# TensorE no longer waits on its own semaphore in an attention-and-FFN block on one core

## Chip, core and metric

The kernel runs on one core of a Trainium2 chip. The metric is device time in microseconds (us); the median of three runs of the kernel before is 1126.47 us (1125.41 to 1128.68).

## What is computed

A pre-norm transformer block for one sequence of 2048 tokens, width 512, 32 heads of 16, and an FFN of 1792. Inputs and output are bf16.

```
h   = x + softmax((q k^T) * 16**-0.5) v @ wo     # q, k, v = split(layernorm(x) @ wqkv)
out = h + (gelu(z @ w_gate) * (z @ w_up)) @ w_down   # z = layernorm(h), gelu by tanh
```

## The kernel before, in words

**Queues and waits.** `Plan` records each engine's instructions in order. A buffer key has a last writer and its readers, each a pair of engine and count; an instruction that writes the key depends on all of them. `_waits_for` turns these into waits on the engines' progress semaphores and leaves out what the engine has waited for already. This holds for the engine's own earlier instructions too: a matmul that writes a PSUM bank (key `("pb", b)`) which an earlier matmul wrote waits until TensorE's own semaphore (`prog_pe`) shows that matmul as done. `group_begin` and `group_end` move the waits of a group of matmuls to its first one.

**The order.** `Sched` sets the order of every queue while the program is built: it plays the kernel with assumed durations (`TMM` for a 512-column matmul, `TTR` for a transpose, `TQK` and `TPV` for a step of scores and of P·V) and always takes the stream whose next operation can start first, within `LOOK` by priority. `_ready` adds `LAT` after the last operation that is depended on, also where that is one of the same engine.

**The steps.** The work is 32 units (4 chunks of 512 queries x 8 groups of 4 heads), each of 64 tiles of 128 keys x 512 queries, 2048 tiles in all.
- `qk` (recorded at L1147, tile names `QT,KT`): steps of three tiles into PSUM banks 0 to 2 and of two tiles into banks 3 and 4, in turn. A step waits until ScalarE has read the tiles that stood in its banks.
- `exps` (L1153): one exponential on ScalarE for each step: "wide", 1536 columns, for three tiles, "narrow", 1024, for two; 410 wide and 409 narrow ones. A wide and a narrow one together are called a pair here: five tiles.
- `pv` (L1147, `PT,VA`): four matmuls for four tiles, added up in bank 5 (`PVB`) over the 16 key steps of a unit. `ofin` copies that bank out (VectorE, `OA`, L1342), transposes it in two halves (L1346) and divides.
- Dense work in banks 6 and 7: projections (L1146) with transposes (L1229), per chunk the output projection with layer norm (`post`, L1383 to L1407), then `gates`, `ups` and `downs` (L1146). A projection, gate or up is two recorded operations of two matmuls on one bank; a down is 14 matmuls in five operations on one bank.
- Gelu of chunks 0 to 2: VectorE copies the gate (L1431), GpSimd does three operations (L1433 to L1435), ScalarE the tanh (L1441), VectorE two more. In chunk 3, after the last exponential, ScalarE does the whole gelu (L1447). That chunk's post, gates, ups and downs are called the tail.
- `fill` (L1510 to L1523): matmuls of zeros, put in where the plan sees TensorE idle and the columns of a running account (`RATE` per us) are owed. Most add zeros to bank 5, so a fill and a P·V step are writers of the same bank.

A second program with its own plan (`max_path`) stands behind a branch and is not run here.

Of the kernel before, what the change touches and what calls it, by code (L numbers as in the profile page):

```python
# [15 lines left out]
class Plan:  # L16
# [47 lines left out]
    def _waits_for(self, e, deps, extra=()):  # L64
        need = {}
        for (k, v) in list(deps) + list(extra):
            if k == e.name and v > e.count:
                continue
            if v > need.get(k, 0):
                need[k] = v  # L70
        waits = []
        for k, v in need.items():
            if e.known.get(k, 0) >= v:
                continue
            e.known[k] = v
            waits.append((k, v))
        self.n_waits += len(waits)
        return waits
# [800 lines left out]
class Sched:  # L879
# [30 lines left out]
    def _ready(self, op):  # L910
# [9 lines left out]
        if isinstance(op, Op):  # L920
            for k in op.writes:
# [3 lines left out]
                for tok in P.readers.get(k, ()):  # L925
                    r = max(r, self.done[tok])
        return r + LAT

# [7 lines left out]
    def _emit(self, op, start):  # L936
# [4 lines left out]
        for tok in extra:  # L941
            start = max(start, self.done[tok] + LAT)
        self.now = max(self.now, start)
# [64 lines left out]


IDLE = 90000  # L1010
LAT = 0.08
LOOK = 0.12
NRING = 30
NG = 3
TMM, TTR, TTR32, TQK, TPV = 0.24, 0.12, 0.26, 0.34, 0.33
SLOTS = ((0, 3), (3, 2))
PVB = 5
DENSE = (6, 7)
# [572 lines left out]
```

## Time and profile before

| | |
|---|---|
| median of the runs | 1126.47 us |
| profiled execution, its own time | 1128.3 us |
| its span, first to last instruction | 1126.6 us |
| first exponential starts, last one ends | 29.47 and 1054.66 us |
| busy share of the span: TensorE, ScalarE, VectorE, GpSimd | 90%, 88%, 23%, 16% |

The profiled execution lies 1.8 us above the median and 1.7 us above its own span. Times in rows count from the start of the span. "Idle before" at the end of a row is what the engine stood still ahead of that instruction, with the instruction that ended the wait. PE is TensorE's matmuls, PEld its weight loads, ACT ScalarE, DVE VectorE, POOL GpSimd.

### The profile page before, as it was taken

The numbers are of one execution on the slowest core, as the hardware profiler recorded it, in microseconds if no ns is written. First come the engines' busy times: TensorE is split into PE (matmuls) and PEld (weight loads), VectorE is DVE, ScalarE is ACT, GpSimd is POOL, SyncE is SP. The second block draws the span as 40 slices with busy tenths as digits, with TensorE's granted clock in tenths as the row PEclk, the third lists the DMA queues.
The fourth block names the chain that finished last, engine by engine and source line by source line (L and its number), as shares of the span: only waits on it lengthen the run. The fifth ranks groups of instructions, "written<-read, shape, count | busy, mean of one in ns | idle before, by whom it ended". The sixth has DMA issues, their size and how long they took to land.

```text
span 1126.6 us, 15044 instructions
## 1 busy us (share of the span) xinstructions
PE 1017.5 (90%) x6105; PEld 298.4 (26%) x6220; DVE 257.5 (23%) x462; ACT 987.4 (88%) x897; POOL 181.0 (16%) x191
## 2 busy tenths in 40 slices
PE   7899999898998998999899999899999998998887
PEld 2222222222222222222222222222222222222222
DVE  5343600000355200000245300000256200000332
ACT  3599999999999999999999999999999999999420
POOL 6500000000067200000058300000058200000000
PEclk9799999999999999999999999999999999999999
DMA  4000140000000000000000000000000000000000
GB/s 149 1 1 1 50 166 1 1 1 1 1 1 1 10 29 1 1 1 1 1 1 1 10 29 1 1 1 1 1 2 1 10 29 1 1 1 1 1 1 22
DMA packets 12847, 14.96 MB, mean 13 GB/s; under 512 B 1760, under 2 KB 11744, under 8 KB 12768
## 3 DMA queue, kind: packets, MB, share of 16 engines
q1 hardware_dynamic: 12768, 13.90, 3.7%
q8 instruction: 51, 0.84, 0.3%
q14 instruction: 28, 0.23, 0.1%
HBM read 11.80 MB, written 2.10 MB: 12 GB/s over the span
## 4 chain that ended last, share of the span: by engine, by line
PE 76%; POOL 8%; issue 6%; ACT 5%; DVE 2%; POOLq 0%; ACTq 0%; DVEq 0%
PE pbank L1147 34%; PE pbank L1513 23%; PE pbank L1146 15%; ACT PT L1153 5%; POOL w_sb L1435 3%; POOL w_sb L1433 2%; POOL w_sb L1434 2%; PE pbank L1523 2%; PE pbank L1346 2%; POOL xn_sb L1222 1%; DVE OA L1342 1%; DVE g_sb L1431 0%; PE pbank L1405 0%; PE pbank L1383 0%; DVE VA L1282 0%
## 5 line engine op out<-in xcount | busy, mean ns | idle before, releaser
L1153 ACT ACTIVATE PT<-pbank 128x1536 bf16<-128x1536 f32 (+1 forms) x819 | 949.4, 1245 | 55.4 <-PE pbank L1147 52.0
L1147 PE MATMUL pbank<-QT,KT 32*128 32x512 bf16 x2048 | 316.5, 385 | 19.5 <-ACT PT L1153 9.9
L1513 PE MATMUL pbank<-ones_bf,zero_bf 128*128 128x512 bf16 x707 | 275.4, 389 | 48.4 <-PE pbank L1147 15.3
L1147 PE MATMUL pbank<-PT,VA 128*17 128x512 bf16 x2048 | 202.1, 385 | 4.1 <-PE pbank L1147 0.8
L1342 DVE COPY OA<-pbank 128x512 f32<-128x512 f32 x32 | 22.1, 690 | 530.2 <-PE pbank L1147 530.2
L1147 PEld LDWEIGHTS pbank<-QT,KT 32*128 32x128 bf16 x2048 | 77.7, 91 | 240.2 <-issue 139.7
L1513 PEld LDWEIGHTS pbank<-ones_bf,zero_bf 128*128 128x128 bf16 x776 | 74.4, 96 | 246.5 <-PE pbank L1513 141.9
L1399 POOL TENSOR_SCALAR rstd_95<-mv_94 128x1 f32<-128x1 f32 x16 | 3.6, 224 | 834.8 <-DVE mv_94 L1397 834.8
L1147 PEld LDWEIGHTS pbank<-PT,VA 128*17 128x17 bf16 x2048 | 49.7, 87 | 124.4 <-PE pbank L1513 59.0
L1146 PE MATMUL pbank<-wd_sb,GUT 128*128 128x512 bf16 x213 | 59.2, 382 | 2.9 <-PE pbank L1147 0.6
L1435 POOL TENSOR_TENSOR w_sb<-w_sb,g_sb 128x512 f32<-128x512 f32 x42 | 55.5, 1321 | 3.5
L1433 POOL TENSOR_TENSOR w_sb<-g_sb 128x512 f32<-128x512 f32 x42 | 46.1, 1097 | 39.2 <-DVE g_sb L1431 39.1
L1447 ACT ACTIVATE w_sb<-pbank 128x512 f32<-128x512 f32 x14 | 8.4, 597 | 38.8 <-PE pbank L1146 38.8
L1146 PE MATMUL pbank<-xnT,wqkv_sb 128*128 128x512 bf16 x123 | 37.7, 391 | 1.7 <-DVE xnT L1236 0.5
L1442 DVE SCALAR_TENSOR_TENSOR w_sb<-w_sb,g_sb 128x512 f32<-128x512 f32 x42 | 33.7, 802 | 23.7 <-ACT w_sb L1441 23.3
L1431 DVE COPY g_sb<-pbank 128x512 f32<-128x512 f32 x42 | 28.9, 689 | 36.3 <-PE pbank L1146 36.3
L1434 POOL TENSOR_SCALAR w_sb<-w_sb 128x512 f32<-128x512 f32 x42 | 33.5, 797 | 3.7
L1467 DVE SCALAR_TENSOR_TENSOR GUT<-pbank,w_sb 128x512 bf16<-128x512 f32 x42 | 28.7, 688 | 23.3 <-PE pbank L1146 23.2
L1441 ACT ACTIVATE w_sb<-w_sb 128x512 f32<-128x512 f32 x42 | 26.7, 636 | 7.0 <-POOL w_sb L1435 6.9
L1346 PE MATMUL pbank<-ident_77,OA 128*128 128x128 f32 x128 | 27.9, 300 | 2.3 <-DVE OA L1342 2.1
L1523 PE MATMUL pbank<-ones_bf,zero_bf 128*128 128x512 bf16 x69 | 26.9, 393 | 2.5 <-DVE GUT L1467 1.0
L1270 DVE TENSOR_SCALAR QT<-pbank,qmask 128x512 bf16<-128x512 f32 x31 | 23.2, 750 | 7.9 <-PE pbank L1146 6.8
(99 smaller groups left out, 485.6 us busy)
## 6 DMA issues: line engine op xcount, KB each, us to landing
xres<-in_A_x_dram SPq DMA_DIRECT2D x16, 128.0 KB, 2.4
out_dram<-out_sb SPq DMA_DIRECT2D x16, 128.0 KB, 1.7
wg_sb<-in_B_w_gate_dram SPq DMA_DIRECT2D x1, 1792.0 KB, 8.8
wu_sb<-in_B_w_up_dram SPq DMA_DIRECT2D x1, 1792.0 KB, 12.9
wd_sb<-in_B_w_down_dram SPq DMA_DIRECT2D x1, 1792.0 KB, 17.5
x_sb<-in_A_x_dram SPq DMA_DIRECT2D x3, 512.0 KB, 7.7
wqkv_sb<-in_A_wqkv_dram SPq DMA_DIRECT2D x2, 384.0 KB, 8.0
x_sb<-in_A_x_dram SPq DMA_DIRECT2D x2, 256.0 KB, 3.2
```

Of the source, the lines that this page charges most:

```text
L1146: return lambda e: e.matmul(o, l, r, start=start, stop=stop)
L1147: return lambda e: e.matmul(o, l, r, start=start, stop=stop, tile_position=tile)
L1153: return lambda e: e.activation(out=o, in_=i, func=func, **kw)
L1342: yield Op("dve", 0.61, lambda e: e.tensor_copy(out=OA[:, par, :], in_=pbank[:, PVB, :]), reads=[("pb", PVB)], writes=[("OA", par)])
L1346: yield Op("pe", 2 * TTR32, cols=256, fns=[lambda e, qt=qt: e.transpose(out=pbank[:, b, 128 * qt:128 * qt + 128], in_=OA[:, par, 128 * qt: ...
L1431: yield Op("dve", 0.61, lambda e: e.tensor_copy(out=gs, in_=pbank[:, b, :]), reads=[("pb", b)], writes=[("g", i)], extra=dE)
L1433: yield Op("pool", 1.05, lambda e: e.tensor_tensor(out=ws, in0=gs, in1=gs, op=ALU.mult), reads=[("g", i)], writes=[("w", i)])
L1434: yield Op("pool", 0.62, lambda e: e.tensor_scalar(out=ws, in0=ws, scalar1=GA, scalar2=1.0, op0=ALU.mult, op1=ALU.add), reads=[("w", i)], ...
L1435: yield Op("pool", 1.27, lambda e: e.tensor_tensor(out=ws, in0=ws, in1=gs, op=ALU.mult), reads=[("w", i), ("g", i)], writes=[("w", i)])
L1442: yield Op("dve", 0.6, lambda e: e.scalar_tensor_tensor(out=ws, in0=ws, scalar=1.0, in1=gs, op0=ALU.add, op1=ALU.mult), reads=[("w", i), ( ...
L1513: fill_op = Op("pe", TMM, lambda e: e.matmul(pbank[:, PVB, :], zero_bf[:], ones_bf[:], start=False, stop=False, skip_group_check=True), re ...
L1523: op = Op("pe", TMM, lambda e: e.matmul(pbank[:, b, :], zero_bf[:], ones_bf[:], start=True, stop=True), reads=["zero_bf", "ones_bf"], writ ...
```

## The change

TensorE's dependencies on its own earlier matmuls are skipped when waits are made; other engines still wait on their own earlier work as before. And four of the planner's assumed durations get other values, which changes the order of the queues.

```diff
@@ Plan._waits_for
         for (k, v) in list(deps) + list(extra):
-            if k == e.name and v > e.count:
+            if k == e.name and (v > e.count or k == "pe"):
                 continue
@@ constants
-LAT = 0.08
+LAT = 0.12
-TMM, TTR, TTR32, TQK, TPV = 0.24, 0.12, 0.26, 0.34, 0.33
+TMM, TTR, TTR32, TQK, TPV = 0.225, 0.11, 0.26, 0.33, 0.33
```

In the part of the program that runs, 1570 matmuls carry a wait on `prog_pe` before, 1471 of them no other; after, none does. By line: 765 and 38 fills (L1513, L1523), 441 of L1147, 242 of L1146, 47 halves of L1346, 25 of L1510, 12 others. The number of waits on ScalarE stays at 836, that on VectorE goes from 250 to 258. Fills into bank 5 go from 776 to 811, other fills (L1523) from 73 to 74; all other instructions are the same in number.

TensorE's queue in the middle of the program, where there is no dense work (`prog_act` is ScalarE's semaphore). Before:

```order
L1147 MATMUL pbank<-QT,KT 128x512 [waits prog_act]
L1147 MATMUL pbank<-QT,KT 128x512
L1513 MATMUL pbank<-ones_bf,zero_bf 128x512 [waits prog_pe] x3
L1147 MATMUL pbank<-QT,KT 128x512 [waits prog_act]
L1147 MATMUL pbank<-QT,KT 128x512 x2
L1147 MATMUL pbank<-PT,VA 17x512 [waits prog_pe]
L1147 MATMUL pbank<-PT,VA 17x512 x3
```

After:

```order
L1147 MATMUL pbank<-QT,KT 128x512 [waits prog_act]
L1147 MATMUL pbank<-QT,KT 128x512
L1513 MATMUL pbank<-ones_bf,zero_bf 128x512 x3
L1147 MATMUL pbank<-QT,KT 128x512 [waits prog_act]
L1147 MATMUL pbank<-QT,KT 128x512 x2
L1147 MATMUL pbank<-PT,VA 17x512 x4
L1513 MATMUL pbank<-ones_bf,zero_bf 128x512
```

Nothing moved in this piece but the waits: each of the three fills and the P·V step waited for the matmul ahead of it.

TensorE's queue in the tail, gates and ups of chunk 3. Before:

```order
L1146 MATMUL pbank<-hnT_c_71,wg_sb 128x512 [waits prog_act]
L1146 MATMUL pbank<-hnT_c_71,wg_sb 128x512
L1146 MATMUL pbank<-hnT_c_71,wg_sb 128x512 [waits prog_pe]
L1146 MATMUL pbank<-hnT_c_71,wg_sb 128x512
L1146 MATMUL pbank<-hnT_c_71,wu_sb 128x512 x2
L1146 MATMUL pbank<-hnT_c_71,wu_sb 128x512 [waits prog_dve]
```

After:

```order
L1146 MATMUL pbank<-hnT_c_71,wg_sb 128x512 [waits prog_act]
L1146 MATMUL pbank<-hnT_c_71,wg_sb 128x512 x3
L1146 MATMUL pbank<-hnT_c_71,wu_sb 128x512 x2
L1146 MATMUL pbank<-hnT_c_71,wu_sb 128x512 [waits prog_dve]
L1146 MATMUL pbank<-hnT_c_71,wu_sb 128x512
```

The order is the same; the second half of a gate waited for the first. In the tail as a whole 60 such waits stood: 14 in gates, 3 in ups, 16 in downs, 5 in the output projection, 20 at fills and 2 at P·V steps.

ScalarE's queue where the first chunk's tanh stand among the exponentials. Before:

```order
L1441 ACTIVATE w_sb<-w_sb 128x512
L1153 ACTIVATE PT<-pbank 128x1024
L1153 ACTIVATE PT<-pbank 128x1536
L1153 ACTIVATE PT<-pbank 128x1024
L1441 ACTIVATE w_sb<-w_sb 128x512
L1153 ACTIVATE PT<-pbank 128x1536
L1153 ACTIVATE PT<-pbank 128x1024
L1153 ACTIVATE PT<-pbank 128x1536
L1441 ACTIVATE w_sb<-w_sb 128x512
```

After:

```order
L1441 ACTIVATE w_sb<-w_sb 128x512
L1153 ACTIVATE PT<-pbank 128x1536
L1153 ACTIVATE PT<-pbank 128x1024
L1153 ACTIVATE PT<-pbank 128x1536
L1441 ACTIVATE w_sb<-w_sb 128x512
L1153 ACTIVATE PT<-pbank 128x1024
L1153 ACTIVATE PT<-pbank 128x1536
L1441 ACTIVATE w_sb<-w_sb 128x512
```

The tanh stand at other places among the exponentials, mostly with two or three between them (before, two to four); the order of exponentials among themselves, GpSimd's order and the order of transfers are unchanged.

## Rows read from the trace of the kernel before

**Rows 1.** The page, busy time and share of each engine, number of instructions.
```profile
PE 1017.5 (90%) x6105; PEld 298.4 (26%) x6220; DVE 257.5 (23%) x462; ACT 987.4 (88%) x897; POOL 181.0 (16%) x191
```
**Rows 2.** Windows: stretch, length, busy per engine (instructions), granted clock, DMA share, GB/s.
```profile
30.30:44.00 13.70, 10.49 (x45) 2.80 (x47) 2.75 (x6) 6.48 (x6) 13.45 (x9) 0.50 0.01 2
...
60.00:1050.00 990.00, 907.45 (x5622) 263.96 (x5723) 206.32 (x353) 944.67 (x842) 143.43 (x150) 1.00 0.03 10
```
**Rows 3.** Timeline of ScalarE: start, length, instruction, count, idle before it.
```profile
240.92 4.62 ACT L1153 ACTIVATE PT<-pbank 128x1536 bf16<-128x1536 f32 x4 [0.24 <-PE pbank L1147]
...
245.78 6.95 ACT L1153 ACTIVATE PT<-pbank 128x1536 bf16<-128x1536 f32 x6 [0.24 <-PE pbank L1147]
...
561.12 17.27 ACT L1153 ACTIVATE PT<-pbank 128x1536 bf16<-128x1536 f32 x15 [0.35 <-PE pbank L1147]
```
**Rows 4.** Timeline of TensorE over the same two pairs, 240.48 to 245.34 us.
```profile
240.48 0.39 PE L1147 MATMUL pbank<-QT,KT 32*128 32x512 bf16 x3
240.80 0.39 PE L1147 MATMUL pbank<-PT,VA 128*17 128x512 bf16 x4
...
241.13 0.39 PE L1147 MATMUL pbank<-QT,KT 32*128 32x512 bf16 x2
...
241.45 1.29 PE L1513 MATMUL pbank<-ones_bf,zero_bf 128*128 128x512 bf16 x3
241.90 0.10 PEld L1513 LDWEIGHTS pbank<-ones_bf,zero_bf 128*128 128x128 bf16 x1 [0.35 <-PE pbank L1513]
...
242.67 0.39 PE L1147 MATMUL pbank<-QT,KT 32*128 32x512 bf16 x3
...
242.99 0.39 PE L1147 MATMUL pbank<-PT,VA 128*17 128x512 bf16 x4
...
243.46 0.39 PE L1513 MATMUL pbank<-ones_bf,zero_bf 128*128 128x512 bf16 x1
...
245.34 0.64 PE L1147 MATMUL pbank<-QT,KT 32*128 32x512 bf16 x5
```
**Rows 5.** Waits: engine, line, whom it waited for, us in total, times, longest.
```profile
PEld pbank L1513 <- PE pbank L1513: 141.9, 430, 0.4
...
ACT PT L1153 <- PE pbank L1147: 52.0, 133, 5.8
...
ACT w_sb L1441 <- POOL w_sb L1435: 6.9, 15, 0.6
```
**Rows 6.** Timeline of ScalarE, first exponentials, at the start of the attention.
```profile
29.47 2.36 ACT L1153 ACTIVATE PT<-pbank 128x1536 bf16<-128x1536 f32 x2 [5.75 <-PE pbank L1147]
34.02 1.45 ACT L1153 ACTIVATE PT<-pbank 128x1536 bf16<-128x1536 f32 x1 [2.18 <-PE pbank L1147]
...
54.69 6.88 ACT L1153 ACTIVATE PT<-pbank 128x1536 bf16<-128x1536 f32 x6 [3.44 <-PE pbank L1147]
```
**Rows 7.** Timeline of ScalarE where chunk 0's gelu runs.
```profile
342.09 0.63 ACT L1441 ACTIVATE w_sb<-w_sb 128x512 f32<-128x512 f32 x1 [0.50 <-POOL w_sb L1435]
342.62 2.35 ACT L1153 ACTIVATE PT<-pbank 128x1024 bf16<-128x1024 f32 x2
345.47 0.63 ACT L1441 ACTIVATE w_sb<-w_sb 128x512 f32<-128x512 f32 x1 [0.50 <-POOL w_sb L1435]
```
**Rows 8.** Timeline of all engines, from the last exponentials to the downs.
```profile
1050.95 3.71 ACT L1153 ACTIVATE PT<-pbank 128x1536 bf16<-128x1536 f32 x3 [0.29 <-PE pbank L1147]
...
1057.40 1.73 PE L1523 MATMUL pbank<-ones_bf,zero_bf 128*128 128x512 bf16 x4
...
1093.57 1.26 PE L1146 MATMUL pbank<-hnT_c_71,wg_sb 128*128 128x512 bf16 x4
...
1094.67 1.03 PE L1146 MATMUL pbank<-hnT_c_71,wu_sb 128*128 128x512 bf16 x4
...
1112.75 0.76 PEld L1146 LDWEIGHTS pbank<-wd_sb,GUT 128*128 128x128 bf16 x5 [0.55 <-PE pbank L1146]
...
1116.71 0.76 PEld L1146 LDWEIGHTS pbank<-wd_sb,GUT 128*128 128x128 bf16 x5 [0.55 <-PE pbank L1146]
```

## The prediction

> **What bounds the kernel now.** I read the page's shares first, then the windows, then ScalarE's timeline, TensorE's timeline of the same microseconds, and last the waits. The shares name two candidates: TensorE 90% and ScalarE 88% [rows 1]. Almost all of the time is the attention: the first exponential starts at 29.47 us and the last one ends at 1050.95 + 3.71 = 1054.66 us [rows 8]. In the middle 990 us ScalarE is busy for 944.67 us [rows 2], and it has 800 exponentials and 42 tanh to do there (842 instructions), so it looks like the bound. Its timeline says it isn't quite. Where nothing holds it up, 15 exponentials take 17.27 us; without the last, wide one (1.45 us alone [rows 6]) that is seven pairs in 15.82 us, 2.26 us a pair [rows 3]. In the stretches without dense work two pairs take 4.62 us, then 0.24 us of standing still for TensorE, and the next two start 245.78 - 240.92 = 4.86 us after the first: 2.43 us a pair [rows 3]. TensorE's rows of the same 4.86 us (240.48 to 245.34) are full from end to end [rows 4]: steps of scores and P·V that start 0.32 or 0.33 us after one another, three fills that take from 241.45 to 242.67, a fill that starts 0.47 us after a P·V step. So TensorE sets the pace there, and ScalarE waits for it 133 times, 52.0 us in all [rows 5].
>
> Why TensorE is full is in its weight loads: the load of a fill stands still for 0.35 us after the fill ahead of it [rows 4], and fills waited for fills 430 times, 141.9 us [rows 5]. That is the wait that the change removes.
>
> **What one removed wait is worth to TensorE.** In the tail four matmuls with one such wait among them take 1.26 us, four without take 1.03 [rows 8]: 0.23 us for a wait, and (1.03 - 0.39) / 3 = 0.21 us from matmul to matmul without one. A fill behind a P·V step starts 0.47 us after it, where a step of scores starts 0.33 us after it [rows 4]: 0.14 us. Behind a step of scores a fill starts after 0.32 us, no more than any change of kind costs, so there the wait was free. In the two pairs of rows 4 there are six fills (three, one, and, not shown, two more behind a third P·V step that follows the scores after the fill at 243.46): three fills behind fills, 3 x 0.23, and two behind P·V, 2 x 0.14, make 0.97 us. TensorE then needs 4.86 - 0.97 = 3.89 us for what ScalarE takes 4.52 us for, and ScalarE becomes the bound, with 0.63 us to spare on TensorE. 1570 waits at 0.14 to 0.23 us are 220 to 361 us of TensorE's time, but only what ScalarE or the end waits for counts.
>
> A stall can't be hidden behind another in one case that matters: could the wide step be late because of its banks? A wide exponential takes 1.45 us [rows 6]; TensorE's scores start at 240.48 and ScalarE follows at 240.92, 0.44 us later [rows 3, 4]. 1.45 + 0.44 = 1.89 us, plus the release, is under 2.26. The banks leave some 0.3 us.
>
> **Middle, 60 to 1050 us.** ScalarE's own work is 400 x 2.26 = 904 us of exponentials and 42 x 0.53 = 22 us of tanh (342.62 - 342.09 [rows 7]). 990 - 926 = 64 us are lost. GpSimd's share is 6.9 us in 15 waits [rows 5] and some 2 us of overlap lost with them; 55 us are left for TensorE. By another way: of the 133 waits six lie before 60 us (five of 10.9 us in all, the first of 2.18 and the last of 3.44 in rows 6, and 5.75 us ahead of the first exponential, there too), so about 35 us lie here in 127 waits; each also costs 0.10 us of overlap (4.86 - 4.52 - 0.24), 13 us: 48 us. I take 55, since small delays show up as no idle time. The waits' removal alone can't make any operation later, since queues and durations stay; only the new order can. It keeps some delays: in 12 of 409 wide steps more than 1.3 us of TensorE's work stands ahead since the narrow step, counted with 0.21 us a matmul, and at each of 32 unit ends the transposes stand ahead of a wide step and wait for VectorE's copy. I keep 5 us for these; the ends are 0 and half of the 55.
>
> **What is late next.** In the gelu windows of chunks 0 to 2 GpSimd needs 3.38 us from one tanh to the next (342.09 to 345.47), ScalarE only about 2 x 1.13 (half a pair each) + 0.53 = 2.79 us with two exponentials between them [rows 7]. After, there are two or three. Over the first twelve gaps of a chunk these are 29, 29 and 28 exponentials: 39.1, 39.1 and 38.0 us against GpSimd's 40.6, so some 6 us of waiting in three chunks at the least, where the rows of now have 6.9. With TensorE out of the way such waits are no longer swallowed. I add 4 us; the ends are 0 and 39 gaps x 0.59 = 23, less 7 = 16.
>
> **Head.** The five waits of 10.9 us [rows 6] lie where GpSimd's normalisation feeds the transposes and the granted clock is 0.50 [rows 2], the lower of its two levels (1.2 GHz). I take 3 us, between 0 and 6. The warm-up matmuls lose their waits too, but the first exponential waits for GpSimd all the same: nothing.
>
> **Tail.** Gates and ups: 17 waits x 0.23 = 3.9 us. Downs: 16 x 0.23 = 3.7 us; a down now takes 1116.71 - 1112.75 = 3.96 us [rows 8], which is 14 x 0.21 + 4 x 0.23. Both are end to end on the path. Between the halves of the last unit's transposes four fills took 1.73 us [rows 8], where the new order has one: 1.2 us. One wait of the first output projection and those of the fills ahead of the first gate: 0.7 us. Sum 9.5; the ends are 7.6 (gates, ups and downs alone) and 11.
>
> **Sum.** 55 - 5 - 4 + 3 + 9.5 = 58.5 us. From the profiled execution's 1128.3 that is 1069.8; since it lay 1.8 us above the median, 1068 us. The 36 more fills cost 36 x 0.21 = 8 us of TensorE's time, in the 0.63 us per two pairs that it has free; without that cover they would take back 8 us.
>
> **The rivals.**
>
> *ScalarE is the bound already.* The late wide exponentials would then have another cause (banks, release), the middle stays, and only head and tail gain: 1126.5 - 12.5 = 1114 us. Against it: TensorE's full 4.86 us and the 0.3 us that the banks leave. The Trainium skill, Perfetto Trace Analysis, section Identifying the Most-Contended Engine, says that a matmul's busy share is a poor measure of how near TensorE is to its limit and that weight loads' share tells more; by it ScalarE is to be worked on first, and this edit would give little. The trace has 26% for the weight loads and 88% for ScalarE, which speaks for the rule; but it is an average, and the rows of single pairs show ScalarE waiting. Chance 8%.
>
> *Half of the delays stay, or GpSimd paces the gelu windows*: 55 x 0.5 + 16 is 27.5 + 16 lost where I lose 9. One of them alone gives 1068 + 12 to 1068 + 23, so 1080 to 1091; both, 1102. Chance of over 1092: 5%.
>
> *The clock falls, and the kernel is slower.* TensorE, done sooner, stands idle more. It ran at 0.50 from 30.30 to 44.00 us, after it had waited for GpSimd, and at 1.00 through the middle [rows 2]. At half the clock 3.89 us of work for two pairs becomes up to 7.8, TensorE is the bound again, and each us of such a stretch loses 1 - 4.52 / 7.8 = 0.42 us. The gain of 58 is gone once 140 us, a seventh of the middle, run so; at 200 us the time is 1068 + 84 = 1152. Against it: the columns per pair stay (some fills more) and a pair gets shorter, so TensorE does more per us than now. The Trainium skill, TensorE: Matmul & The Clock Gate, Part 1, says that the low clock is the default and that activity lifts it; the trace agrees at the start of the attention (0.50 after waiting). Chance 4%.
>
> *The change does not do what it says.* Matmuls into one bank might stay as far apart without the wait, and the time would stay at 1126. Against it: 0.21 us between two matmuls of a projection's half on one bank [rows 8]. Chance 3%.
>
> **How the numbers follow.** The forecast, TensorE's waits gone and ScalarE the pace, has 80%. Its range goes from 1052 (nothing kept in the middle, +5; no GpSimd loss, +4; head 6, +3; tail 11, +1.5; and 2 us for run-to-run spread: 15.5) up to 1092 (GpSimd or half of the delays, 23). What is left out, under 20%, is the rivals' share and the case that ScalarE's pair gets shorter than the 2.26 us. A measurement of this kernel can tell about 0.3% (3.4 us) from no change. Faster by more: the forecast, the first two rivals: 93%. Same: 3%. Slower: 4%.
>
> **What would show it.** Right: no wait of fills for fills among the waits; in the middle two pairs in 4.5 to 4.6 us with TensorE's score steps waiting on ScalarE; ScalarE's waits on TensorE down from 52 to some 20 us, those on GpSimd up; last exponential near 1006; four matmuls in 1.03 us throughout the gates, a down in 3.0 us. Wrong: 4.86 us for two pairs with gaps on TensorE (the banks), or a granted clock under 1.00 in the middle.

## The result, and the profile after

The changed kernel takes 1063.6 us (median of 4 executions, 1062.85 to 1066.65), the kernel before 1127.4: a ratio of 0.944, with an interval of 0.942 to 0.947. The profiled execution of after took 1062.85 us, 1061.1 of them span; that of before 1128.3 and 1126.6. Four of the ten executions of e2 and two of the five of e3 below, the profiled one of e3 among them (0.50 from 131 to 384 us), show a lower granted clock for long stretches and take 1187 to 1229 us; the ratios and times given leave these out.

First the page's line of busy time, in the form of [rows 1]:

```profile
PE 951.1 (90%) x6139; PEld 288.9 (27%) x6255; DVE 258.6 (24%) x462; ACT 971.7 (92%) x897; POOL 181.6 (17%) x191
```

By the shares nothing seems to have happened to TensorE: 90% then and now. In absolute time it lost 66 us of busy time and ScalarE only 16, so ScalarE's share rose from 88% to 92%. The windows say where. The columns are those of [rows 2]; the stretches are the attention from 60 us to the last exponential's end, and the tail behind it, for after and then for before:

```profile
29.30:60.00 30.70, 26.49 (x158) 8.38 (x161) 11.78 (x21) 22.58 (x20) 14.42 (x9) 0.82 0.01 1
60.00:1002.40 942.40, 858.49 (x5660) 250.96 (x5765) 205.67 (x351) 930.26 (x842) 144.10 (x150) 1.00 0.03 11
1002.40:1061.10 58.70, 49.47 (x246) 22.26 (x251) 25.39 (x49) 9.88 (x17) 3.17 (x8) 1.00 0.04 11
```

```profile
60.00:1054.60 994.60, 911.18 (x5647) 265.14 (x5749) 206.32 (x353) 948.98 (x845) 143.43 (x150) 1.00 0.03 10
1054.60:1126.60 72.00, 58.73 (x245) 19.61 (x249) 25.55 (x49) 9.91 (x17) 3.17 (x8) 0.97 0.03 9
```

From 60 us on ScalarE is now busy for 930.26 of 942.40 us, 98.7%. The stretch is 52.2 us shorter. Of that, 3.6 us had been gained ahead of its start: the 25th exponential starts at 65.40 us, before at 68.99, and ScalarE has 842 instructions left behind 60 us instead of 845. So the middle itself gave 48.7 us. The tail went from 72.0 to 58.7, 13.2 us by the unrounded ends of the last exponential (1054.66 and 1002.42). The three add up to 65.5 us, the difference of the spans.

ScalarE's timeline in the middle, which answers to [rows 3]:

```profile
157.59 59.10 ACT L1153 ACTIVATE PT<-pbank 128x1536 bf16<-128x1536 f32 x52
```

52 exponentials in one piece, with no idle time ahead of any: 26 pairs in 59.10 us, 2.27 us each. TensorE's timeline in that piece, which answers to [rows 4]:

```profile
160.25 0.39 PE L1147 MATMUL pbank<-QT,KT 32*128 32x512 bf16 x2 [0.20 <-ACT PT L1153]
160.57 0.39 PE L1523 MATMUL pbank<-ones_bf,zero_bf 128*128 128x512 bf16 x1
...
162.40 0.59 PE L1513 MATMUL pbank<-ones_bf,zero_bf 128*128 128x512 bf16 x2
162.93 0.39 PE L1147 MATMUL pbank<-QT,KT 32*128 32x512 bf16 x2
...
164.77 0.39 PE L1147 MATMUL pbank<-QT,KT 32*128 32x512 bf16 x2 [0.16 <-ACT PT L1153]
```

From one narrow step of scores to the next but one it is 164.77 - 160.25 = 4.52 us for two pairs, and it is now the score steps that wait, for ScalarE. From the start of the first fill in these rows to the next step it is 0.53 us for two fills (a third ahead of them has a weight load but no matmul record), where three took 1.22. The waits, which answer to [rows 5], whole execution and then ScalarE's from 60 us on:

```profile
PEld pbank L1147 <- ACT PT L1153: 352.1, 731, 1.2
...
PEld pbank L1513 <- issue: 84.6, 372, 0.4
...
ACT PT L1153 <- PE pbank L1147: 20.3, 14, 8.3
```

```profile
ACT w_sb L1441 <- POOL w_sb L1435: 7.1, 17, 0.6
ACT PT L1153 <- PE pbank L1147: 3.9, 8, 2.0
```

No fill waits for a fill any more. ScalarE's waits on TensorE went from 133 to 14, and from 60 us on from 127 (35.3 us) to 8 (3.9 us); those on GpSimd stayed, 6.9 to 7.1 us.

The start of the attention, which answers to [rows 6], and then the tail, which answers to [rows 8]:

```profile
29.30 2.37 ACT L1153 ACTIVATE PT<-pbank 128x1536 bf16<-128x1536 f32 x2 [8.31 <-PE pbank L1147]
33.42 1.45 ACT L1153 ACTIVATE PT<-pbank 128x1536 bf16<-128x1536 f32 x1 [1.75 <-PE pbank L1147]
...
51.62 10.61 ACT L1153 ACTIVATE PT<-pbank 128x1536 bf16<-128x1536 f32 x9 [2.60 <-PE pbank L1147]
```

```profile
1002.47 0.39 PE L1147 MATMUL pbank<-PT,VA 128*17 128x512 bf16 x4 [0.41 <-ACT PT L1153]
...
1015.65 2.12 PE L1523 MATMUL pbank<-ones_bf,zero_bf 128*128 128x512 bf16 x9
...
1019.42 2.76 PE L1146 MATMUL pbank<-hnT_c_71,wg_sb 128*128 128x512 bf16 x11
...
1037.13 1.03 PE L1146 MATMUL pbank<-hnT_c_71,wg_sb 128*128 128x512 bf16 x4
...
1043.61 12.25 PE L1146 MATMUL pbank<-wd_sb,GUT 128*128 128x512 bf16 x55
```

Four matmuls of a gate take 1.03 us, as those of an up did already, and the 56 of the downs 12.25 (one record is missing): 14 of them 3.0 us. Two rows of before, from the same places, show what the prediction had not priced there:

```profile
1055.93 0.39 PE L1147 MATMUL pbank<-PT,VA 128*17 128x512 bf16 x4
...
1075.98 4.47 PE L1146 MATMUL pbank<-hnT_c_71,wg_sb 128*128 128x512 bf16 x11
```

Before, the last P·V step came 1.27 us after the last exponential's end (1054.66), behind three fills; now it comes 0.05 us after it (1002.42). And the first eleven matmuls of the gates took 4.47 us: 0.7 more than now for three waits, and 1.0 more for the clock, which was 0.50 (1.2 GHz) from 1074.8 to 1078.2 us:

```profile
1074.80:1078.20 3.40, 3.22 (x8) 0.81 (x8) 0.30 (x1) 0.03 (x1) 0.00 (x0) 0.50 0.03 7
```

### The profile page after: what moved, and what is told of

Its sections match the earlier page's. It is cut to its first block, busy times and chain, and to the rows that moved or that the text cites. A ratio compares the mean times of both kernels' runs of the same rounds, so it can differ in the third digit from the quotient of the medians.

```text
span 1061.1 us, 15019 instructions
## 1 busy us (share of the span) xinstructions
PE 951.1 (90%) x6139; PEld 288.9 (27%) x6255; DVE 258.6 (24%) x462; ACT 971.7 (92%) x897; POOL 181.6 (17%) x191
## 4 chain that ended last, share of the span: by engine, by line
ACT 32%; PE 28%; issue 23%; POOL 12%; DVE 2%; ACTq 0%; POOLq 0%; DVEq 0%
ACT PT L1153 32%; PE pbank L1146 13%; PE pbank L1147 12%; POOL w_sb L1435 5%; POOL w_sb L1433 4%; POOL w_sb L1434 3%; PE pbank L1513 2%; POOL xn_sb L1222 1%; PE pbank L1346 1%; DVE g_sb L1431 0%; DVE QT L1270 0%; DVE stats_93 L1396 0%; ACTq L152 0%; PE pbank L1523 0%; DVE VA L1282 0%
## 5 line engine op out<-in xcount | busy, mean ns | idle before, releaser
L1153 ACT ACTIVATE PT<-pbank 128x1536 bf16<-128x1536 f32 (+1 forms) x819 | 934.1, 1406 | 21.4 <-PE pbank L1147 20.3
L1147 PE MATMUL pbank<-QT,KT 32*128 32x512 bf16 x2048 | 319.5, 386 | 69.6 <-ACT PT L1153 48.6
L1513 PE MATMUL pbank<-ones_bf,zero_bf 128*128 128x512 bf16 x743 | 226.3, 383 | 7.3 <-issue 7.0
L1147 PE MATMUL pbank<-PT,VA 128*17 128x512 bf16 x2048 | 201.0, 385 | 1.2 <-ACT PT L1153 0.4
L1147 PEld LDWEIGHTS pbank<-QT,KT 32*128 32x128 bf16 x2048 | 78.0, 91 | 380.8 <-ACT PT L1153 350.7
L1513 PEld LDWEIGHTS pbank<-ones_bf,zero_bf 128*128 128x128 bf16 x811 | 57.0, 97 | 99.7 <-issue 84.6
L1147 PEld LDWEIGHTS pbank<-PT,VA 128*17 128x17 bf16 x2048 | 49.1, 87 | 118.1 <-issue 109.6
L1146 PE MATMUL pbank<-wd_sb,GUT 128*128 128x512 bf16 x215 | 56.4, 381 | 0.9 <-issue 0.8
L1146 PE MATMUL pbank<-xnT,wqkv_sb 128*128 128x512 bf16 x121 | 35.5, 394 | 1.0 <-issue 0.5
L1346 PE MATMUL pbank<-ident_77,OA 128*128 128x128 f32 x128 | 27.3, 298 | 0.9 <-DVE OA L1342 0.9
L1222 POOL TENSOR_SCALAR xn_sb<-x_sb,mv,rstd 128x512 bf16<-128x512 bf16 x12 | 24.8, 2079 | 0.5 <-issue 0.3
L1146 PEld LDWEIGHTS pbank<-wd_sb,GUT 128*128 128x128 bf16 x224 | 17.6, 98 | 26.3 <-issue 12.2
```

What stands on the lines that cost most here:

```text
L1146: return lambda e: e.matmul(o, l, r, start=start, stop=stop)
L1147: return lambda e: e.matmul(o, l, r, start=start, stop=stop, tile_position=tile)
L1153: return lambda e: e.activation(out=o, in_=i, func=func, **kw)
L1222: lambda e, t=t: e.tensor_scalar(out=xn_sb[:, t % 8, :], in0=x_sb[:, t, :], scalar1=mv[:, t, 0:1], scalar2=rstd[:, t:t + 1], op0=ALU.subtr ...
L1346: yield Op("pe", 2 * TTR32, cols=256, fns=[lambda e, qt=qt: e.transpose(out=pbank[:, b, 128 * qt:128 * qt + 128], in_=OA[:, par, 128 * qt: ...
L1513: fill_op = Op("pe", TMM, lambda e: e.matmul(pbank[:, PVB, :], zero_bf[:], ones_bf[:], start=False, stop=False, skip_group_check=True), re ...
```

## Experiments

Theory: the self-waits, those of fills above all, made TensorE the pace of the middle; without them it is ScalarE, and the tail is shorter by its own waits. Rivals: the new order brings the gain; the clock decides; half of the removal would have been enough.

### Which part of the edit

**e1**, the waits gone, the planner's numbers as before:

```diff
-LAT = 0.12
+LAT = 0.08
-TMM, TTR, TTR32, TQK, TPV = 0.225, 0.11, 0.26, 0.33, 0.33
+TMM, TTR, TTR32, TQK, TPV = 0.24, 0.12, 0.26, 0.34, 0.33
```

> Edit: the waits are gone as in the change, the five numbers of the planner (LAT, TMM, TTR, TQK) stand as before. Theory (TensorE's waits on itself paced ScalarE, the new order is worth little): 1060 to 1075 us, ScalarE in the middle at 2.26 us a pair, its waits on TensorE near 20 us. Rival (the new order of the queues brings a good part): 1090 us or more. Between 1075 and 1090 the order has a share worth naming.

Measured: 1061.8 us, ratio 0.941 (0.937 to 0.944). **e2** is the other half, the new numbers with all waits:

```diff
-            if k == e.name and (v > e.count or k == "pe"):
+            if k == e.name and v > e.count:
```

> Edit: the planner's numbers are the new ones, so the order is that of the changed kernel, and every wait of TensorE on itself is back (1589 in the first program). Theory: 1120 to 1133 us, two pairs again in some 4.86 us, fills waiting for fills some 140 us. Rival (the order brings it): 1095 us or less. What this run and the one with the waits alone leave over or count twice is what the two parts do only together.

Measured: ratio 1.000 (0.998 to 1.002). Its waits of fills for fills:

```profile
PEld pbank L1513 <- PE pbank L1513: 153.9, 472, 0.4
```

The waits carry the whole gain; the order carries none that can be measured. It moves time about, though. The four profiles make a square, cut here at the start of the 25th exponential, where the clock is back at 1.00 in all of them, and at the end of the last one (us):

| | up to the 25th | from there to the last | tail |
|---|---|---|---|
| old order, waits (before) | 69.0 | 985.7 | 71.9 |
| old order, no waits (e1) | 68.4 | 933.1 | 60.8 |
| new order, waits (e2) | 66.1 | 989.5 | 69.6 |
| new order, no waits (after) | 65.4 | 937.0 | 58.7 |

Without the waits the middle is 52.5 us shorter in either order, the tail some 11 and the head 0.6. The new order makes the head 3 us shorter and the tail 2, and the middle 3.9 longer. Each row is one execution (e1's is the longest of its four), so 1 or 2 us between two rows prove little by themselves.

One likely reason in the tail can be read: e1 has no fills between the transposes at 1015.04 and those at 1018.32, its clock is 0.50 from 1018.1 to 1021.5, and its first eleven gate matmuls, without a wait among them, take 3.49 us where the changed kernel, with nine fills at 1015.65 in that place, needs 2.76.

```profile
1020.00 3.49 PE L1146 MATMUL pbank<-hnT_c,wg_sb 128*128 128x512 bf16 x11
```

### Which waits

In **e3** only the fills wait for TensorE's own matmuls, in **e4** everything but the fills; the order is that of the changed kernel in both.

```diff
+        deps, self.isfill = self._deps(reads, writes), "zero_bf" in reads
...
-            if k == e.name and (v > e.count or k == "pe"):
+            if k == e.name and (v > e.count or (k == "pe" and not self.isfill)):     # e3
+            if k == e.name and (v > e.count or (k == "pe" and self.isfill)):         # e4
```

> Edit: the changed kernel, in which only the fills (L1513, L1523; 853 instructions) wait for TensorE's own matmuls; all other waits on itself stay away. Theory (in the middle the fills' waits alone make the 0.97 us per two pairs, the tail's gain is that of the projections): the middle goes back to 4.8 us for two pairs, last exponential near 1048 to 1055 us, the tail stays at about 59 us: 1105 to 1115 us. Rival (half of the waits away is enough, since TensorE has spare time): 1080 us or less.

Measured for e3: ratio 0.988 (0.984 to 0.992), executions of 1114.2, 1116.1 and 1116.9 us, the middle one 1 us above the expected range. Rows of its profile from a stretch at a granted clock of 1.00:

```profile
558.69 4.62 ACT L1153 ACTIVATE PT<-pbank 128x1536 bf16<-128x1536 f32 x4 [0.29 <-PE pbank L1147]
563.54 4.63 ACT L1153 ACTIVATE PT<-pbank 128x1536 bf16<-128x1536 f32 x4 [0.22 <-PE pbank L1147]
568.40 4.62 ACT L1153 ACTIVATE PT<-pbank 128x1536 bf16<-128x1536 f32 x4 [0.23 <-PE pbank L1147]
```

At full clock two pairs take 4.85 us again, as in [rows 3], with ScalarE waiting each time. The fills' waits alone restore the old pace of the middle: 1116.1 - 1063.6 = 52 us. "Half is enough" is out.

> Edit: the changed kernel, in which everything but the fills waits for TensorE's own matmuls (953 instructions, 219 of them projection matmuls with that wait alone), and the fills don't. Theory: the middle keeps ScalarE's pace of 2.26 us a pair outside of dense work, the tail gives back 7.6 us or more (gates, ups and downs, 33 x 0.23 us), dense work in the middle 1 to 15 us: 1070 to 1086 us. Rival (P.V steps that wait for a fill ahead of them on bank 5 cost as much as the fills' own waits did): 1095 us or more.

Measured for e4: 1077.5 us, ratio 0.955 (0.952 to 0.958), so the other waits cost 13.9 us. The last exponential ends at 1008.5, which makes the tail 67.1 us, 8.4 longer than in the changed kernel; the other 5.6 us lie in the attention. Rows of its tail, for the gates and downs, and ScalarE's waits from 60 us on:

```profile
1032.78 1.26 PE L1146 MATMUL pbank<-hnT_c,wg_sb 128*128 128x512 bf16 x4
...
1056.88 13.43 PE L1146 MATMUL pbank<-wd_sb,GUT 128*128 128x512 bf16 x46
```

```profile
ACT w_sb L1441 <- POOL w_sb L1435: 7.5, 16, 0.8
ACT PT L1153 <- PE pbank L1147: 6.6, 18, 2.0
```

ScalarE's waits on TensorE stay small although 953 of TensorE's instructions wait for TensorE: they lie where it has time to spare. The two parts, 52 and 14 us, add up to 66, against the 64 that the whole change gave: they overlap hardly at all, since the one is the middle's and the other mostly the tail's.

### What the fills and the clock are worth

**e5** is the changed kernel without fills, **e6** the kernel before without fills:

```diff
-    sch.fill = fill
+    sch.fill = None
```

> Edit: the changed kernel without fills (L1513 and L1523 are never issued; nothing that the output needs is left out). It prices the rival in which the clock falls. Two pairs then need 3.89 - 6 x 0.21 = 2.63 us of TensorE at full clock, 5.26 at half. Theory (the fills are what holds the granted clock at 1.00): stretches of the middle at 0.50, ScalarE waits for TensorE there, two pairs in 5.0 to 5.5 us, tail longer too: 1100 to 1180 us, slower than the changed kernel by 40 us or more. Rival (the clock holds without them): 1055 to 1066 us, ScalarE still at 2.26 us a pair.

> Edit: the kernel before, with all its waits, without fills. Theory: no fill is left to wait, so at full clock two pairs would need 4.86 - 6 x 0.21 - 0.97 = 2.6 us of TensorE and ScalarE would be the bound: 1065 to 1085 us if the granted clock stays at 1.00; 1110 to 1190 us, within 15 us of the changed kernel without fills plus its tail waits, if it falls to 0.50. Rival (the stall is not the fills' but that of the banks or of the other waits): 1120 to 1130 us at a clock of 1.00.

Measured: e5 1090.7 us, ratio 0.966 (0.962 to 0.971); e6 1109.6 us, ratio 0.983 (0.979 to 0.988). The clock fell in both, as the first theory of each had it, but the times lie below what the theory made of that: 27 us over the changed kernel instead of 40 or more, and 1109.6 just under 1110. A stretch without dense work in each (columns as above), e5 and then e6:

```profile
660.00:780.00 120.00, 99.72 (x538) 19.86 (x534) 5.49 (x12) 117.35 (x105) 0.00 (x0) 0.50 0.00 1
```

```profile
660.00:780.00 120.00, 99.04 (x534) 20.74 (x530) 5.49 (x12) 117.00 (x105) 0.00 (x0) 0.50 0.00 1
```

At half the clock ScalarE is still busy for 117 of 120 us. TensorE's rows of e5 say why; here it is at 0.50 too:

```profile
163.80 0.61 PE L1147 MATMUL pbank<-QT,KT 32*128 32x512 bf16 x3 [0.50 <-ACT PT L1153]
164.34 0.61 PE L1147 MATMUL pbank<-PT,VA 128*17 128x512 bf16 x4
164.88 0.60 PE L1147 MATMUL pbank<-QT,KT 32*128 32x512 bf16 x2
```

A step starts 0.54 us after the one ahead, where it is 0.32 at full clock: 1.7 times, not twice. The expectation had doubled the whole 2.63 us. Four steps of scores and two or three of P·V take 6.5 x 0.54 = 3.5 us, still under 4.52. What e5 loses lies in the attention, 995.5 us from 30.13 to 1025.66 against 973.1, in 46 waits for TensorE (38.0 us against 20.3), and 4.4 us in the tail. From 60 us on there are 40 of these waits, 22.6 us; 18 of them, 12.9 us, lie in three short stretches where a chunk's dense work sets in while the clock is at 0.50 for a part (278 to 303, 530 to 542 and 778 to 806 us; mean clock 0.81, 0.57 and 0.68). So over half of this waiting lies there, and little in long stretches like the one shown.

The two runs together turn the sign of the fills. Without the self-waits they bring 1090.7 - 1063.6 = 27 us, by the clock that they hold up; with the self-waits they cost 1127.5 - 1109.6 = 18 us, clock and all. The kernel before was slower than its own version without fills.

**e9**, fewer fills (651 for 885):

```diff
-RATE = 1250
+RATE = 1000
```

> Edit: the changed kernel with RATE 1000 instead of 1250; the planner then issues 651 fills instead of 885. It tells whether the fills that the change added (36 of them) and the others are free, as the prediction's cover of 0.63 us per two pairs has it, and how near the clock is to falling. Theory (fills lie in time that TensorE has to spare, and the clock needs most of them): the same 1061 to 1066 us where the granted clock holds at 1.00, and up to 1090 us, the time without any fill, if it falls to 0.50 between the dense chunks. Rival (fills still stand in ScalarE's way): 1050 to 1059 us at a clock of 1.00.

Measured: 1062.5 us, ratio 0.942 (0.940 to 0.945), the same as the changed kernel, with a clock of 1.00 throughout the middle. A quarter of the fills can go without effect on either: the fills lie in time that TensorE has to spare. That the clock needs "most of them" is not shown: 651 hold it, and fewer were not tried.

### What is late next

**e7** takes work from GpSimd's gelu: `w * GA + 1`, then `* g`, become one operation on VectorE.

```diff
-        yield Op("pool", 0.62, lambda e: e.tensor_scalar(out=ws, in0=ws, scalar1=GA, scalar2=1.0, ...
-        yield Op("pool", 1.27, lambda e: e.tensor_tensor(out=ws, in0=ws, in1=gs, op=ALU.mult), ...
+        yield Op("dve", 0.7, lambda e: e.scalar_tensor_tensor(out=ws, in0=ws, scalar=1.0 / GA, in1=gs, op0=ALU.add, op1=ALU.mult), ...
...
-        ... activation(out=ws, in_=ws, func=ACT.Tanh, scale=GC)
+        ... activation(out=ws, in_=ws, func=ACT.Tanh, scale=GC * GA)
```

> Edit: the changed kernel, in which the second and third GpSimd operation of each gelu (L1434, L1435; 42 of each) become one on VectorE (w + 1/GA) * g, and the tanh's scale takes the factor GA. It measures the term 'GpSimd paces the gelu windows'. Theory (the waits on GpSimd are end to end on ScalarE's path): those waits (8.3 us in 17) go, and with them up to as much of lost overlap: 1050 to 1060 us. Rival (the exponentials behind them only move, or VectorE's port and queue delay others): 1061 to 1068 us.

Measured: 1058.75 us, ratio 0.939 (0.934 to 0.943), 4.9 us less than the changed kernel. ScalarE's tanh waits, 7.1 us in 17, are now

```profile
ACT w_sb L1441 <- DVE w_sb L1434: 2.4, 5, 0.6
```

4.7 us of waits and 4.9 of time: these waits seem to lie end to end on the path, with little lost overlap. The two ratios' intervals just overlap; all four of its executions (1058.6 to 1062.45) lie below all four of the changed kernel's. (The 8.3 in the expectation was a misreading: that is the longest wait of the exponentials.)

**e8** moves the normalisation of chunks 1 to 3 to VectorE:

```diff
-            eng = "dve" if c == 0 else "pool"
-            yield Op(eng, 0.35 if c == 0 else 0.77,
+            eng = "dve"
+            yield Op(eng, 0.35,
```

> Edit: the changed kernel, in which the normalisation of chunks 1 to 3 (L1222, 12 instructions) runs on VectorE as that of chunk 0 does, instead of GpSimd, where one takes 2.07 us. Theory (GpSimd's normalisation sets the first exponential at 29.3 us and the 8 us of gaps behind it): first exponential at 22 to 26 us, gaps of the head under 5 us, 1052 to 1060 us, and the low clock of 23 to 40 us is shorter. Rival (TensorE's queue or the low clock sets them): 1061 to 1067 us.

Measured: 1053.7 us, ratio 0.933 (0.929 to 0.937), 9.9 us less than the changed kernel. ScalarE's first rows:

```profile
26.36 7.05 ACT L1153 ACTIVATE PT<-pbank 128x1536 bf16<-128x1536 f32 x6 [6.59 <-PE pbank L1147]
34.50 6.89 ACT L1153 ACTIVATE PT<-pbank 128x1536 bf16<-128x1536 f32 x6 [1.08 <-PE pbank L1147]
43.98 16.14 ACT L1153 ACTIVATE PT<-pbank 128x1536 bf16<-128x1536 f32 x14 [2.60 <-PE pbank L1147]
```

The gaps behind the first exponential go from 8.1 to 3.7 us; the first exponential comes 2.9 us earlier in this execution, the longest of the four (1056.9), and just outside the expected 22 to 26. GpSimd's normalisation did set the head, as far as this run can tell: the granted clock, 0.50 from 23.2 to 40.2 us in the changed kernel, is 1.00 here from 25.6 us to the end of the attention, and no run separates the clock's share of the gain. **e10** has both moves:

> Edit: the changed kernel with both moves to VectorE together: the normalisation of chunks 1 to 3, and the second and third operation of each gelu as one. Alone the two gave 9.9 and 4.9 us. Theory (they lie in different stretches of ScalarE's path, head and gelu windows, and add): 1046 to 1052 us. Rival (VectorE's queue now delays evacuations that TensorE waits for): 1053 us or more.

Measured: 1048.5 us, ratio 0.930 (0.928 to 0.933). 15.1 us less than the changed kernel, where the two alone gave 14.8: they add. In its profile the first exponential starts at 23.78 us, and the granted clock is 1.00 from 20 us to 994. This version beats both kernels.

## Why the prediction held, step by step

It said 1068 us, between 1052 and 1092, faster with 93%; 1063.6 came. The sum was 58.5 us against 65.5 measured between the profiled executions:

| Term | Predicted (ends) | Measured |
|---|---|---|
| middle, after what is kept and GpSimd | 55 - 5 - 4 = 46 | 48.7 |
| head | 3 (0 to 6) | 3.6 |
| tail | 9.5 (7.6 to 11) | 13.2 |

**The bound.** Right: two pairs in 4.52 us, score steps waiting for ScalarE, ScalarE's waits on TensorE 20.3 us ("some 20"), last exponential's end at 1002.4 ("near 1006"). e3 shows the mechanism apart from the rest: the fills' waits alone bring the 4.85 us back.

**The middle's size.** The square of profiles splits it. The end of the waits gave 52.5 us there, so of the two ways of counting the 55 that was taken was nearer than the 48. The new order took 3.9 back, where 5 was kept for its late steps; ScalarE has 8 waits on TensorE left behind 60 us (3.9 us), in e1 with the old order 4 (0.9 us). What was mis-sized is "GpSimd's waits up by 4 us": they went from 6.9 to 7.1. The count of exponentials between two tanh gave waiting of some 6 us as the least with TensorE out of the way, and the rows agree with that; the error was to add to it. So the middle gave 2.7 us more than the sum had.

**The tail** lies 2.2 us above its upper end, and that is a step left out. Gates and ups gave 29.15 - 24.19 = 4.96 us (predicted 3.9), downs 21.47 - 17.49 = 3.98 (3.7), the part ahead of the gates 21.3 - 17.0 = 4.3 (1.9). By the square the end of the waits gave some 11 us of it and the new order 2. The waits of gates, ups and downs were sized well: e4 gives back 8.4 us in the tail for them. Left out were the last P·V step behind three fills, each waiting for the one ahead (1.2 us), and the stretch at half the clock at the first gates (1.0 us there, and part of the 0.8 us by which the last transposes reach them sooner), which is gone. e1's row points to the new order for that, whose nine fills stand where e1 has none. So do e2 and e4, which have the new order and the gates' waits: there the clock is 1.00, and the eleven take 3.45 and 3.47 us, 0.7 for the three waits and 1.0 less than before.

```profile
1025.98 3.47 PE L1146 MATMUL pbank<-hnT_c,wg_sb 128*128 128x512 bf16 x11
```

But the new order doesn't ensure it: in e8's profile, with the same order there, the clock is 0.50 from 1005.2 to 1008.7 us, earlier in the tail. What makes the clock fall in one execution's tail and not in another's stays open. The page's clock row of before has a 9 in that slice, a mean over 28 us; a window of a few us over the first gates shows the stretch.

**The head** came out in size by luck. The prediction took 3 of the 10.9 us of waits there without working the share out. By the square of profiles the end of the waits gave 0.6 or 0.7 us of the 3.6 and the new order the rest, though one execution each is thin for that. That the head hangs on GpSimd's normalisation, as the prediction says, e8 bears out.

**The rivals.** "ScalarE is the bound already" fell with the time and with the 52 exponentials without a wait. The Trainium skill's rule that was set against the change (Perfetto Trace Analysis, Identifying the Most-Contended Engine) pointed to ScalarE by the shares, 88% against 26% of weight loads; the measurement decides otherwise here: an edit on TensorE alone gave 5.6%, and the weight loads' share is 27% now. A sum over the execution can't show that one engine is late for the other by 0.34 us in every two pairs. "Half of the delays stay" fell with 8 waits left, "GpSimd paces the gelu windows" with its 7.1 us, and "the change does not do what it says" with the gates' 1.03 us. "The clock falls" didn't happen: 1.00 from 60 us to the end, and ahead of that 0.50 from 23.2 to 40.2 us, before from 30.4 to 44.0. Its price was sized too high in one respect, since a step doesn't double at half the clock (e5), and its mechanism is real: without fills the clock does fall, and costs 27 us. That the Trainium skill calls the low clock the default and has activity lift it (TensorE: Matmul & The Clock Gate, Part 1) agrees with e5 and e6: 0.50 in the stretches without dense work, and 1.00 there in the profiles of before and after, which have fills.

**Free cover.** The 36 more fills cost nothing that can be measured, as e9 shows for 234 fewer.

## What to carry to other kernels

Where an engine's own queue already keeps an order, look for waits of the engine on itself, and price one from two rows that differ in it alone; then ask in which stretch the engine is late for the one that paces it, since 0.23 us counts only there. Work that is put in to fill time (here matmuls that hold the clock) is to be measured against its own absence, and again after each change around it: it cost 18 us in one version and brought 27 in the next. When the bound has moved to one engine, its remaining waits name the next edits, one by one.

## Not expected of the hardware

A step of scores or of P·V starts 0.54 us after the one ahead at a granted clock of 0.50 and 0.32 us after it at 1.00. Matmuls of 512 columns and of one tile shape differ by as much. In e8's tail, at 0.50, four fills and the matmul behind them start 0.43 us after one another (1005.29 to 1007.00 in four steps); at 1.00 nine fills in the changed kernel's tail do so every (2.12 - 0.39) / 8 = 0.22 us.

```profile
1005.20:1008.70 3.50, 3.50 (x13) 1.31 (x12) 2.17 (x6) 0.00 (x0) 0.79 (x2) 0.51 0.00 0
```

```profile
1005.29 1.91 PE L1523 MATMUL pbank<-ones_bf,zero_bf 128*128 128x512 bf16 x4
1007.00 1.85 PE L1146 MATMUL pbank<-wo_sb,OnT 128*128 128x512 bf16 x4
```

What a change of tile shape adds is about 0.11 us in these rows at either clock (0.54 - 0.43 and 0.32 - 0.21): it doesn't scale with the clock.

Two fills ahead of a step of scores take 0.53 us from the first's start, 0.21 for a fill behind which a fill stands and 0.32 for one behind which the shape changes.
